# Preparing the first head pair of an attention kernel differently: sums by tensor, scaling on VectorE, joined turns, values loaded elsewhere, other dummies

## The chip, the cores and the metric

The kernel runs on one core of one Trainium2 chip. The metric is the device time of one execution in microseconds (us); lower is better. Each version is run several times and the median is taken. One further execution is recorded by the hardware profiler, and all views of the profile come from that one.

A core has a matrix engine (TensorE, PE in the profile, with PEld for its weight loads), VectorE (DVE), ScalarE (ACT), GpSimd (POOL) and SyncE (SP), which here only issues DMAs. Each engine works off its own instructions in program order and waits on semaphores for the others.

## The reference

An attention with normalised queries and keys (batch 8, 12 heads, 448 tokens, head dimension 64) is followed by a gated feed-forward block on 3584 tokens (model width 768, inner width 1536). Everything is float32.

```
q_n = q / sqrt(mean(q*q) + 1e-6) * g_q        # k_n likewise, with g_k
scores = q_n @ k_n.T / 8                      # per batch and head
attn   = softmax(scores)
x      = (attn @ v) as rows of 12*64 = 768
out    = (silu(x @ w_gate) * (x @ w_val)) @ w_out
```

The three weight matrices arrive in double precision, and the kernel converts them itself.

## The kernel before, in words

The program has a fast path (`fast`) and a general one that is entered only for unusual gains and is not used here. The fast path works on 48 pairs of heads: a pair is two heads of one batch. The first 12 pairs ("early", two batches) are done first, in an attention phase of their own. Then come four blocks of the feed-forward part, each for two batches. The blocks use a scheme with fewer products than the plain matrix product, so that inputs and weights are first combined into "sides" (line 1128 and 1132 for the inputs). The pairs of the next block are mixed into the present block.

In the attention phase each pair passes these steps. A pair's number is m; x is 0 for queries and 1 for keys.

- `load` (L748): one DMA each for queries and keys, rows of 112 partitions by 2 heads by 256 numbers, issued by SP. Four such tiles exist, so pair m+2 waits until pair m's tiles are free.
- `load_values` (L771, L774): four DMAs for the values, issued by SP. Two buffers.
- `square` (L784): ACT squares each tensor, 112x512.
- `summed` (L804): one DVE reduction, 112x1024 to 112x16, for both tensors.
- `inverse_root` (L698, L699 on ACT; L704 to L706 on DVE): Ln and Exp give an estimate of one over the root, and three small DVE operations improve it.
- `scale` (L843): two GpSimd products, 112x512, keys first.
- `turn` (L869): four PE transposes for each tensor into one PSUM tile of two banks (`st`).
- `drain`: keys on DVE (L875), queries on ACT with the gains `gg` as scale (L877).
- `scores` (L927) on PE and `exps` (L942) on ACT, in four parts j = 3, 0, 1, 2, where part 3 is half as wide. Two PSUM tiles `st` are shared by these and the turns.
- `weighted` (L1003) and `total` (L1034) on PE, then `copy_sums` (L1092, ACT), `join` (L1095, DVE), `invert` (L1070, L1072), `exchange` (L1085, ACT), `spread` (L1089) and `divide` (L1098).

Beside this, the first seven of 24 weight tiles are converted. A conversion (`convert`) has five DMAs (L1215, L1217), two ACT passes of 128x1152 (L1225, L1229), nine DVE operations in three parts (L1246, L1252, L1258), twelve GpSimd operations (L1279, L1282) and a DMA back to device memory (L1307).

The order of the instructions is made by a planner in plain Python, the class `Order`. Each step is added as a piece with its engine, a listed cost, a due time (`when`), the pieces that it comes after, the buffers that it takes and uses, and sometimes `early`, the time ahead of its due time from which it may start. The due time less a `rank` is its key. The early pairs have rank 60, the first weight conversions rank 20. `run` keeps a clock for each engine by the listed costs. It takes next the piece that can start first, with the key deciding between near ones, and emits it. So a changed cost or dependency can change the order of everything after it. DMAs are modelled with eight outstanding places. In the constants `LEAD` is 10.6 and `PAIR` 8.97: pair m has `base` = 10.6 + 8.97 m and `ready` = `base` - 8.97.

Ahead of the planned part, `fast` emits some steps by hand (from L1683): memsets on GpSimd, the table load on ACT (L570), four small gain loads on GpSimd's queue (L1692, L1693), the identity for the transposes, and a planned DVE product for the gains (L1697). A small check of the gains runs before that (L1748 to L1753). Pair 0's first square emits three extra PE products that nothing reads ("dummies", L787).

The dependencies that the planner does not model are found when the instructions are built: an instruction waits for earlier ones that touch the same memory, and for a PSUM tile the whole tile counts as seen in the trace.

Of the kernel before, what the change touches and what calls it, by code (L numbers as in the profile page):

```python
# [13 lines left out]
ALU = mybir.AluOpType  # L14
AX = mybir.AxisListType
# [477 lines left out]
def fast(  # L493
# [41 lines left out]
    nc = tc.nc  # L535
    B, H, S, D = q.shape
    DM = H * D
    DFF = moe_w_gate.shape[1]
    P = 128
    NJ = 4  # L540
    Q = S // 2
# [12 lines left out]
    VALUE_MOVES = [transfer(384, 256)] * 2 + [transfer(128, 256)] * 2  # L554
    NATURAL = (0, 1, 2, 3, 4, 5, 6, 7, 8, 9, 10, 11)
    R = S // NJ
# [9 lines left out]
        rr=4, ws=2, **{x + str(i): 1 for x in "vw" for i in range(6)},  # L566
# [5 lines left out]
    order = Order(dict(BUFS, bits=1), dict(logarithms=load_tables))  # L572
    tiles = {}
# [112 lines left out]
    GAIN = 2.0**24  # L686

    SCALE = 2.0**8
# [34 lines left out]
    def attention(m):  # L723
# [14 lines left out]
        def add(*what, **more):  # L738
            return order.add(*what, rank=rank, **more)
# [33 lines left out]
            for p in (0, D):  # L773
                nc.sync.dma_start(x[ds(p, D), NJ - 1], rows)  # L774

        load_v = add("SP", 2.4, ready - 16.0, load_values, takes=[("v", m)], moves=VALUE_MOVES, early=25.0)

        def square(x):
            if x == 0:
                take("t", m, [R, 2, 2 * NJ * D] if natural else [P, 2, NC, C])  # L780
            of = tiles["qk", (m, x)]
            if natural:
                of = of.rearrange("p h f -> p (h f)")
            nc.scalar.activation(tiles["t", m][:, x], of, AF.Square)  # L784
            if m == 0 and x == 0:
                for _ in range(3):
                    nc.tensor.matmul(banks[0], ident[0:R], of, start=True, stop=True)  # L787

        squares = []
        for x in range(2):  # L790
# [5 lines left out]
                )  # L796
            )


        def summed():  # L800
            if natural:
# [19 lines left out]
        def both():  # L821
# [2 lines left out]
                ss[:, 0], ss[:, 0], D * 1e-6, ss[:, 1], op0=ALU.add, op1=ALU.add  # L824
            )

        sums = add(
            "DVE", 1.45 if natural else 1.08, ready - 17.0, summed, after=squares, uses=[("t", m)], takes=[("ss", m)]
        )
        if not natural:  # L830
            sums = add("ACT", 0.88, ready - 16.0, swap, after=[sums], uses=[("ss", m)])
# [7 lines left out]
        def scale(x):  # L839
            if natural:  # L840
                split = dict(h=2, j=NJ, d=D)
                rr = tiles["rr", m][:, ts(x, 2 * NJ)].rearrange("p (h j one) -> p h j one", h=2, one=1)
                nc.gpsimd.tensor_tensor(  # L843
                    out=tiles["t", m][:, x].rearrange("p (j h d) -> p h j d", **split),
                    in0=tiles["qk", (m, x)].rearrange("p h (j d) -> p h j d", d=D),
                    in1=rr.to_broadcast([R, 2, NJ, D]), op=ALU.mult,
                )
                return
            rr = tiles["rr", m][:, ts(x, NC)].rearrange("p (c one) -> p c one", one=1)
            nc.gpsimd.tensor_tensor(  # L850
                out=tiles["t", m][:, x], in0=tiles["qk", (m, x)], in1=rr.to_broadcast([P, NC, C]),
                op=ALU.mult,
            )

        scaled = [
            add(
                "POOL", 0.98, ready - 9.0, lambda x=x: scale(x), after=[rr], port=True,
                uses=[("qk", (m, x)), ("t", m), ("rr", m)],
            )
            for x in (1, 0)  # L860
# [3 lines left out]
        def turn(x):  # L864
            if x:
                take("st", (m, "turned"), [P, 2, TB])
            turned = tiles["st", (m, "turned")][:, x]
            for j in range(NJ):
                nc.tensor.transpose(turned[:, ts(j, R)], tiles["t", m][:, x, ts(j, P)], ident[0:R, 0:R])  # L869

        def drain(x):
            turned = tiles["st", (m, "turned")][:, x, 0:S].rearrange("p (j r) -> p r j", j=NJ)
# [16 lines left out]
        kt = qt = None  # L889
        if natural:  # L890
            of_turned = ("st", (m, "turned"))
            for x in (1, 0):
                qt = add(
                    "PE", 0.4, ready - 6.0, lambda x=x: turn(x), after=[scaled[1 - x], qt],
                    uses=[("t", m)] + [of_turned] * (1 - x), takes=[of_turned] * x, mode="full",
                )
                kt = kt or qt
            kt = add(
                "DVE", 0.62, ready - 5.0, lambda: drain(1), after=[kt], takes=[("KT", m)],
                uses=[of_turned],  # L900
            )
            qt = add(
                "ACT", 0.63, ready - 5.0, lambda: drain(0), after=[qt, gains], takes=[("QT", m)],
                uses=[of_turned],
            )
        kt = kt or add(
            "DVE", 0.64, ready - 6.0, lambda: transpose(1), after=scaled[:1], takes=[("KT", m)],
            uses=[("t", m)],
# [771 lines left out]

    nc.gpsimd.memset(many, SCALE)  # L1683
    nc.gpsimd.memset(little, D * 1e-6 * GAIN**-2)
    nc.gpsimd.memset(halves, 0.0)
    for x in range(2):
        nc.gpsimd.memset(halves[ds(D * x, D), x], SCALE)
    load_tables()
    order.mode["ACT"] = "logarithms"
    for t, x in ((gq2, g_q), (gk2, g_k)):  # L1690
        col = x.rearrange("(d one) -> d one", one=1)
        nc.gpsimd.dma_start(t[0:64, :], col)  # L1692
        nc.gpsimd.dma_start(t[64:128, :], col)  # L1693
    make_identity(nc, ident)
    gains = order.add(
        "DVE", 0.2, 9.0,
        lambda: nc.vector.scalar_tensor_tensor(  # L1697
            out=gg, in0=gq2, scalar=8.0 * GAIN**-2, in1=gk2, op0=ALU.mult, op1=ALU.mult
        ),
        early=0.0,  # L1700
    )
    for m in range(EARLY):
        attention(m)
    first = [(up_weights, i) for i in range(4 * NG)] + [(down_weights, i) for i in range(2 * NG)]
# [83 lines left out]
```

## Time and profile before

| What | Value |
|---|---|
| time, three runs | 1462.16, 1462.22, 1463.76 us (median 1462.22) |
| profiled execution, its own time | 1464.89 us |
| its span, first to last instruction | 1463.1 us |
| PE busy | 1429.7 us (98%) |
| DVE busy | 881.6 us (60%) |
| ACT busy | 605.4 us (41%) |
| POOL busy | 398.3 us (27%) |
| granted PE clock, mean | 0.994 |
| DMA | 193.28 MB, mean 132 GB/s |

How to read the views that follow. A line of a group or of the timeline has the start in us and the busy time in us (timeline), the engine, the line of the code, the operation, the tile written and the tiles read, the shapes, and the count after an x. In square brackets stands how long the engine idled just before, and who released it. In the table by stage each row is a stretch of time, with each engine's busy time and, in brackets, its number of instructions; then the granted PE clock as a share of the full one, the share of time the DMA engines were busy, and the rate in GB/s. A line of the waits gives the waiting engine and line, whom it waited for, the total in us, how often, and the longest. "issue" means that nothing in the profile explains the idle time. Matmul ends are modelled.

### The profile page before, as it was taken

What the parts mean: (1) busy time and instruction counts of PE and PEld (TensorE: products, weight loads), DVE (VectorE), ACT (ScalarE), POOL (GpSimd) and SP (SyncE); (2) the same over time, 40 slices, a digit from 0 to 9 for tenths busy, and PEclk for the clock granted to TensorE, in tenths of its full rate; (3) what the DMA queues carried; (4) which work ended last, traced back from release to release, by engine and by line L of the source; (5) the groups of instructions that cost most, each with busy time, mean ns of one, the idle gap of its engine ahead of it and who ended that gap; (6) DMA issues with size and microseconds to landing.
All of it is one profiled execution on the core that took longest, in us unless ns stands there. A gap on an engine that the chain in (4) does not pass through costs nothing.

```text
span 1463.1 us, 19387 instructions
## 1 busy us (share of the span) xinstructions
PE 1429.7 (98%) x6726; PEld 685.1 (47%) x6726; DVE 881.6 (60%) x1493; ACT 605.4 (41%) x1222; POOL 398.3 (27%) x471
## 2 busy tenths in 40 slices
PE   6998999999999999999999999999999999999997
PEld 2443555544444455544444455554444445555553
DVE  3889977867866444446767632365676643432533
ACT  5885543457563221355654222254656322122100
POOL 3555786535343000012434200012344300000000
PEclk9999999999999999999999999999999999999999
DMA  7667998954454523443553532453454452322235
GB/s 209 185 189 254 337 313 285 297 139 92 102 103 96 133 72 109 110 101 87 118 116 71 118 99 75 117 118 84 103 116 87 96 134 73 102 78 81 78 99 108
DMA packets 410415, 193.28 MB, mean 132 GB/s; under 512 B 280004, under 2 KB 390852, under 8 KB 410308
## 3 DMA queue, kind: packets, MB, share of 16 engines
q1 hardware_dynamic: 399040, 190.57, 48.3%
q10 hardware_dynamic: 11140, 1.38, 0.7%
q8 instruction: 55, 0.90, 0.3%
q14 instruction: 52, 0.43, 0.1%
q0 software_dynamic: 128, 0.00, 0.0%
HBM read 157.29 MB, written 34.60 MB: 131 GB/s over the span
## 4 chain that ended last, share of the span: by engine, by line
PE 90%; DVE 3%; ACT 2%; DMA 2%; issue 1%; SPq 1%; POOL 0%; DVEq 0%; ACTq 0%; POOLq 0%
PE mm L1416 25%; PE at L1416 25%; PE mm L1594 23%; PE st L927 8%; PE at L1003 7%; PE st L1034 1%; ACT es L942 1%; PE mm L1034 1%; DMA out_dram<-spare 1%; DMA work<-in_k_dram 1%; DVE xs L1132 0%; PE st L869 0%; DMA xs<-in_moe_w_gate_dram 0%; DVE spare L1642 0%; DVE mm L1252 0%
## 5 line engine op out<-in xcount | busy, mean ns | idle before, releaser
L1416 PE MATMUL mm<-xs,ws 128*128 128x448 f32 x960 | 400.3, 540 | 0.0
L1416 PE MATMUL at<-xs,ws 128*128 128x448 f32 x960 | 400.2, 539 | 0.0
L1416 PEld LDWEIGHTS at<-xs,ws 128*128 128x128 f32 x960 | 182.3, 190 | 178.9 <-issue 174.7
L1416 PEld LDWEIGHTS mm<-xs,ws 128*128 128x128 f32 x960 | 182.4, 190 | 178.8 <-issue 174.1
L850 POOL TENSOR_TENSOR work<-work,rr 128x448 f32<-128x448 f32 x72 | 67.0, 952 | 468.6 <-DVE rr L706 381.9
L1594 PE MATMUL mm<-gt,ws 128*128 128x448 f32 x448 | 176.1, 544 | 0.0
L927 PE MATMUL st<-work 64*64 64x448 f32 (+1 forms) x1536 | 157.6, 517 | 13.7 <-ACT es L942 6.2
L942 ACT ACTIVATE es<-st 128x896 f32<-128x896 f32 x129 | 114.1, 913 | 110.5 <-PE at L1003 94.1
L1594 PE MATMUL mm<-hs,ws 128*128 128x448 f32 x384 | 151.8, 546 | 0.0
L1354 DVE TENSOR_TENSOR gt<-gt,mm 128x448 f32<-128x448 f32 x64 | 39.8, 621 | 184.3 <-PE mm L1416 182.8
L947 POOL TENSOR_TENSOR sums<-es 128x896 f32<-128x896 f32 x36 | 77.5, 2153 | 184.2 <-PE st L1034 111.2
L1594 PEld LDWEIGHTS mm<-gt,ws 128*128 128x128 f32 x448 | 83.5, 190 | 83.2 <-issue 81.7
L1490 ACT ACTIVATE st<-gt 128x448 f32<-128x448 f32 x96 | 52.6, 547 | 164.9 <-DVE gt L1358 82.0
L1352 ACT COPY gt<-mm 128x448 f32<-128x448 f32 x80 | 42.5, 531 | 167.4 <-PE mm L1416 167.2
L1003 PE MATMUL at<-es,v 64*64 64x448 f32 x1032 | 109.0, 538 | 2.6 <-DVE xs L1095 2.6
L1594 PEld LDWEIGHTS mm<-hs,ws 128*128 128x128 f32 x384 | 71.5, 191 | 72.9 <-issue 71.8
L927 PEld LDWEIGHTS st<-work 64*64 64x64 f32 x1536 | 51.9, 136 | 86.8 <-issue 40.1
L1352 ACT COPY v<-at 128x448 f32<-128x448 f32 x96 | 50.9, 530 | 76.4 <-PE at L1416 74.0
L947 POOL TENSOR_TENSOR sums<-sums,es 128x896 f32<-128x896 f32 x36 | 75.2, 2089 | 2.8
L1003 PEld LDWEIGHTS at<-es,v 64*64 64x64 f32 x1032 | 40.1, 134 | 61.5 <-issue 54.5
L784 ACT ACTIVATE work<-work 128x448 f32<-128x448 f32 (+1 forms) x96 | 55.2, 587 | 25.8 <-DMA work<-in_q_dram 17.1
L1354 DVE TENSOR_TENSOR v<-v,at 128x448 f32<-128x448 f32 x64 | 39.7, 621 | 41.2 <-PE at L1416 41.2
(160 smaller groups left out, 1566.9 us busy)
## 6 DMA issues: line engine op xcount, KB each, us to landing
ws<-up_sides SPq DMA_DIRECT2D x32, 1024.0 KB, 5.6
ws<-down_sides SPq DMA_DIRECT2D x16, 1024.0 KB, 5.7
ws<-down_sides SPq DMA_DIRECT2D x28, 512.0 KB, 4.6
ws<-up_sides SPq DMA_DIRECT2D x16, 768.0 KB, 4.8
out_dram<-spare SPq DMA_DIRECT2D x168, 56.0 KB, 2.1
v<-in_v_dram SPq DMA_DIRECT2D x96, 96.0 KB, 2.6
ws<-up_sides SPq DMA_DIRECT2D x32, 256.0 KB, 5.9
ws<-up_sides SPq DMA_DIRECT2D x16, 512.0 KB, 5.8
```

Of the source, the lines that this page charges most:

```text
L784: nc.scalar.activation(tiles["t", m][:, x], of, AF.Square)
L850: nc.gpsimd.tensor_tensor(out=tiles["t", m][:, x], in0=tiles["qk", (m, x)], in1=rr.to_broadcast([P, NC, C]), op=ALU.mult,)
L927: nc.tensor.matmul(st[ds(D * x, D), h, 0:n], tiles["KT", m][rows, ds(P * j + D * of_keys, D)], tiles["QT", m][rows, ds(Q * of_queries, n)] ...
L942: nc.scalar.activation(e, tiles["st", (m, j)][:, :, 0 : S * width(j) // P], AF.Exp)
L947: nc.gpsimd.tensor_tensor(out=to, in0=tiles["e", (m, 0)] if j == 1 else to, in1=e, op=ALU.add)
L1003: nc.tensor.matmul(tiles["at", (m, x)][ds(D * h, D), queries], tiles["v", m][rows, j, h], tiles["e", (m, j)][rows, h], start=j == 0, stop= ...
L1034: nc.tensor.matmul(to[ds(D * h + C * x, C)], halves[:, x] if half else many[:, 0:C], term[:, h, 0:Q] if half else term[:, h, ts(x, Q)], st ...
L1352: nc.scalar.copy(to, ps)
L1354: nc.vector.tensor_tensor(out=to, in0=old, in1=ps, op=ALU.add)
L1416: nc.tensor.matmul(ps(), w[:, which, c, at], xs[:, SLOT[x], c], start=fresh and c == 0, stop=c == NC2 - 1, skip_group_check=True,)
L1490: nc.scalar.activation(take(*act, [P, 2, TB])[:, 0, 0:S], to, AF.Silu)
L1594: nc.tensor.matmul(banks[s][:, 0:S], w[:, s, g, at], where[x][:, g], start=fresh and g == 0, stop=g == NG - 1, skip_group_check=True,)
```

## The change

All of it concerns the start of the program. The diff is complete but for unchanged lines.

- Values: the load of an early pair's values is due at `base` - 2 instead of `ready` - 16, and may start 4 us ahead of that instead of 25.
- Dummies: the three products behind pair 0's first square go. Instead DVE clears half of the tile `more`, and PE multiplies it with itself, four times with 448 columns and once with 224 columns, at the start. A further product of 224 columns follows pair 0's turn of the queries.
- Pair 0's sums of squares are two DVE reductions of 112x512, one for each tensor. Pair 1's reduction must come after pair 0's drain of the keys.
- Pair 0 is scaled by DVE instead of GpSimd, with a listed cost of 0.62 instead of 0.98.
- Pair 0's two turns are one piece, emitted one behind the other.
- The gains' product is two GpSimd operations, emitted by hand behind the memsets and the identity, and no planned piece; GpSimd's memsets come behind its DMA issues.

```diff
-        load_v = add("SP", 2.4, ready - 16.0, load_values, takes=[("v", m)], moves=VALUE_MOVES, early=25.0)
+        load_v = add(
+            "SP", 2.4, base - 2.0 if early else ready - 16.0, load_values, takes=[("v", m)], moves=VALUE_MOVES,
+            early=4.0 if early else 25.0,
+        )
...
             nc.scalar.activation(tiles["t", m][:, x], of, AF.Square)
-            if m == 0 and x == 0:
-                for _ in range(3):
-                    nc.tensor.matmul(banks[0], ident[0:R], of, start=True, stop=True)
...
+        def summed_half(x):
+            if x == 0:
+                take("ss", m, [P, 2, 2 * NC])
+            nc.vector.tensor_reduce(
+                out=tiles["ss", m][0:R, 0, ts(x, 2 * NJ)],
+                in_=tiles["t", m][:, x].rearrange("p (n d) -> p n d", d=D), axis=AX.X, op=ALU.add,
+            )
...
-        sums = add(
-            "DVE", 1.45 if natural else 1.08, ready - 17.0, summed, after=squares, uses=[("t", m)], takes=[("ss", m)]
+        sums = None
+        for x in range(2 if m == 0 else 0):
+            sums = add(
+                "DVE", 0.65, ready - 17.0, lambda x=x: summed_half(x), after=[squares[x], sums],
+                uses=[("t", m)] + [("ss", m)] * x, takes=[("ss", m)] * (1 - x),
+            )
+        sums = sums or add(
+            "DVE", 1.45 if natural else 1.08, ready - 17.0, summed,
+            after=[*squares, clusters.get("turned") if m == 1 else None], uses=[("t", m)], takes=[("ss", m)]
         )
...
-                nc.gpsimd.tensor_tensor(
+                engine = nc.gpsimd if m else nc.vector
+                engine.tensor_tensor(
                     out=tiles["t", m][:, x].rearrange("p (j h d) -> p h j d", **split),
...
-                "POOL", 0.98, ready - 9.0, lambda x=x: scale(x), after=[rr], port=True,
+                "POOL" if m else "DVE", 0.98 if m else 0.62, ready - 9.0, lambda x=x: scale(x),
+                after=[rr], port=True,
...
                 nc.tensor.transpose(turned[:, ts(j, R)], tiles["t", m][:, x, ts(j, P)], ident[0:R, 0:R])
+            if m == 0 and x == 0:
+                warm(Q)
...
-            for x in (1, 0):
+            for xs_of in ((1, 0),) if m == 0 else ((1,), (0,)):
                 qt = add(
-                    "PE", 0.4, ready - 6.0, lambda x=x: turn(x), after=[scaled[1 - x], qt],
-                    uses=[("t", m)] + [of_turned] * (1 - x), takes=[of_turned] * x, mode="full",
+                    "PE", 0.4 * len(xs_of), ready - 6.0, lambda xs_of=xs_of: [turn(x) for x in xs_of],
+                    after=[scaled[1 - xs_of[-1]], qt], mode="full",
+                    uses=[("t", m)] + [of_turned] * (1 - xs_of[0]), takes=[of_turned] * xs_of[0],
                 )
...
+            clusters.setdefault("turned", kt)
...
-    nc.gpsimd.memset(many, SCALE)
-    nc.gpsimd.memset(little, D * 1e-6 * GAIN**-2)
-    nc.gpsimd.memset(halves, 0.0)
-    for x in range(2):
-        nc.gpsimd.memset(halves[ds(D * x, D), x], SCALE)
+    def warm(n):
+        nc.tensor.matmul(banks[0][:, 0:n], more[:, 0, 0:P], more[:, 0, 0:n], start=True, stop=True)
+
+    nc.vector.memset(more[:, 0], 0.0)
+    for n in (S, S, S, S, Q):
+        warm(n)
     load_tables()
...
+    nc.gpsimd.memset(gg, 8.0 * GAIN**-2)
+    nc.gpsimd.memset(little, D * 1e-6 * GAIN**-2)
+    nc.gpsimd.memset(many, SCALE)
+    nc.gpsimd.memset(halves, 0.0)
+    for x in range(2):
+        nc.gpsimd.memset(halves[ds(D * x, D), x], SCALE)
     make_identity(nc, ident)
-    gains = order.add(
-        "DVE", 0.2, 9.0,
-        lambda: nc.vector.scalar_tensor_tensor(
-            out=gg, in0=gq2, scalar=8.0 * GAIN**-2, in1=gk2, op0=ALU.mult, op1=ALU.mult
-        ),
-        early=0.0,
-    )
+    nc.gpsimd.tensor_tensor(out=gg, in0=gq2, in1=gg, op=ALU.mult)
+    nc.gpsimd.tensor_tensor(out=gg, in0=gg, in1=gk2, op=ALU.mult)
+    gains = None
```

## The prediction

> **What bounds the kernel now.** I read the page first: TensorE (PE) is busy 1429.7 of 1463.1 us. So only its 33 us of idle time, and the time it spends at half clock, can be won. I then asked for busy time by stage, cutting where the chain of work that ended last changes its engine.
>
> ```profile
> core 0: us, PE busy (x) PEld busy (x) DVE busy (x) ACT busy (x) POOL busy (x), PEclk, DMA share, GB/s
> 0.00:30.68 30.68, 19.44 (x86) 7.75 (x90) 9.84 (x22) 15.51 (x27) 11.11 (x23) 0.90 0.74 200
> 30.68:97.50 66.82, 65.78 (x821) 31.90 (x813) 53.85 (x112) 59.37 (x112) 36.94 (x59) 1.00 0.67 198
> 97.50:130.20 32.70, 26.76 (x292) 11.72 (x292) 31.07 (x58) 22.27 (x37) 17.71 (x32) 0.95 0.65 214
> 134.72:1463.10 1328.38, 1313.19 (x5473) 631.66 (x5472) 782.73 (x1296) 506.94 (x1041) 328.28 (x353) 1.00 0.48 125
> ```
>
> The start (to 30.68) loses 11.2 us of PE. From there to 97.5 PE is full. From 97.5 to 130.2 VectorE (DVE) is full instead and PE loses 5.9 us. The rest is PE again. What the start loses moves everything behind it, if the DVE stage lets it through. Next I read the timeline of pair 0:
>
> ```profile
> 3.78 1.35 ACT L784 ACTIVATE work<-work 112x512 f32<-112x512 f32 x2 [0.91 <-DMA work<-in_q_dram]
> 5.16 1.22 DVE L804 TENSOR_REDUCE ss<-work 112x16 f32<-112x1024 f32 x1 [0.87 <-ACT work L784]
> 6.81 0.63 ACT L784 ACTIVATE work<-work 112x512 f32<-112x512 f32 x1 [1.68 <-DMA work<-in_q_dram]
> 7.70 0.63 ACT L784 ACTIVATE work<-work 112x512 f32<-112x512 f32 x1 [0.26 <-DMA work<-in_k_dram]
> 8.24 0.29 ACT L698 ACTIVATE rr<-ss,little 112x16 f32<-112x16 f32 x1
> 8.36 1.22 DVE L804 TENSOR_REDUCE ss<-work 112x16 f32<-112x1024 f32 x1 [1.98 <-ACT work L784]
> 9.50 0.17 DVE L704 SCALAR_TENSOR_TENSOR ss<-ss,rr 112x16 f32<-112x16 f32 x1
> 10.23 2.04 POOL L843 TENSOR_TENSOR work<-work,rr 112x512 f32<-112x512 f32 x2 [5.98 <-ACT rr L699]
> 12.37 0.62 DVE L875 COPY work<-st 128x448 f32<-128x448 f32 x1 [2.12 <-PE st L869]
> 13.14 0.98 PE L869 MATMUL st<-ident,work 112*128 112x112 f32 x4 [0.81 <-DVE ss L704]
> 14.16 0.63 ACT L877 ACTIVATE work<-st,gg 128x448 f32<-128x448 f32 x1 [3.99 <-PE st L869]
> 14.85 1.77 PE L927 MATMUL st<-work 64*64 64x224 f32 x12 [0.72 <-ACT work L877]
> ```
>
> Pair 0's sums are ready at 6.38, yet its Ln (L698) stands on ACT behind both squares of pair 1, which wait for their loads, until 8.24. Its improvement (L704) then stands on DVE behind pair 1's reduction until 9.50. The second turn (13.14) starts only 0.15 after the first drain ends (12.99), although its input is ready at 12.27: it waits for that drain's reading of the common PSUM tile. Last, what follows:
>
> ```profile
> 20.28 1.26 ACT L1225 ACTIVATE xs<-xs 128x1152 f32<-128x1152 f32 x1
> 21.43 0.91 ACT L942 ACTIVATE es<-st 128x896 f32<-128x896 f32 x1
> 25.20 0.90 ACT L942 ACTIVATE es<-st 128x896 f32<-128x896 f32 x1
> 26.15 4.76 PE L927 MATMUL st<-work 64*64 64x448 f32 x24 [3.15 <-ACT es L942]
> 27.00 0.65 DVE L704 SCALAR_TENSOR_TENSOR ss<-ss,rr 112x16 f32<-112x16 f32 x1 [0.68 <-ACT rr L699]
> PE at L1003 <- DVE xs L1095: 3.7, 2, 2.6
> ```
>
> Pair 1's scores (26.15) wait for pair 0's last Exp on ACT (25.20), which stands in an ACT queue that runs from 19.75 with one gap of 0.32. Before that ACT idles: 10.17 to 14.16, 14.79 to 15.94, 16.48 to 17.43, 18.35 to 19.75, in all 7.5 us. The last line is PE waiting in the DVE stage for a join (L1095).
>
> [...] the row of L1354 has 621; [...] L804 has 1.22 us. So 512 elements cost an estimated 0.69 us. [...] The timeline has 2.04 us for two, against an estimated 1.38, a ratio of 1.5[...]. [...] L704 takes 0.65 at 27.00, inside GpSimd's 26.58 to 28.62, and 0.17 elsewhere. [...] PE idles from 23.0 to 26.15, and the clock is 0.50 from 24.4 to 31.2; eight transposes (L869) take 1.75 at 17.30 and 0.99 at 31.80 (at 17 the clock column says 1.00; there I go by the durations).
>
> **The change, part by part.** Times are the profiled execution's.
>
> Sums by tensor: one reduction of 1.22 becomes two of 0.69. The first runs beside the second square, so the sums end near 5.86 instead of 6.38. By the planner's costs in the code, Ln now falls between pair 1's two squares: its sums come before the second one's load. Those squares wait for real loads (6.79, 7.68), so Ln starts after the first, near 7.4. Before, the last square's start to Exp's end was 8.78 - 7.70 = 1.08; so 6.81 + 1.08 = 7.89. Gain 0.9; the earlier sums alone are worth nothing here.
>
> Pair 1's reduction put after pair 0's key drain: improvement starts at 7.95 instead of 9.50 and ends at 8.53. Gain 1.55 so far. Behind the new wait on DVE stand that reduction, then pair 1's improvement; GpSimd's scaling of pair 1 waits for them. I get 15.3 instead of 13.62 for it. But pair 1's turn started at 17.30 only, held by PE, so this is covered by 1.6 us. Without cover it costs up to 1.7.
>
> Scaling on DVE: 8.55 to 9.95, two of 0.69, instead of 1.85 for GpSimd's first turn plus the wait. The bounds are 0.62 (planner's cost) and 1.02 (GpSimd's) each. GpSimd does nothing then but two 128x1 products for the gains[...].
>
> Both turns together: they run 9.3 to 11.1 cold (eight took 1.75 in pair 1), or to 10.5 warm. Then the DVE drain, 0.62, and the ACT drain, 0.63, which in pair 1 waits for the DVE one (19.75 after 19.71); with the hand-overs, scores at 12.5 cold, 11.9 warm, against 14.85. Gain 2.3 to 2.9; I take 2.5.
>
> Dummies: four products of 448 and one of 224 columns. The old dummy's 512-column half costs 0.85, so these cost 4 x 1.5 + 0.75 = 6.7, from some 1.2 to 7.9[...]. Turns start at 9.3: hidden by 1.4. The one behind the turns (0.75) is hidden by the drains (1.25). DVE's new memset (not in the trace; between 0.1 and a copy's 0.62) is hidden before 3.66.
>
> Gains on GpSimd: DVE loses 0.16; the gains' last load landed near 8.3 and the ACT drain needs them at 11.2: hidden by 2.9, at nothing. GpSimd's memsets behind its four DMA issues: identity still by 4.5, nothing.
>
> Values: eight DMAs (2.69 to 8.30) leave SP's queue ahead of the first weights; pair 0's four go behind the first weight load's five, pair 1's four behind the second weight load's five and pair 2's queries and keys. Later pairs keep their buffers' release as their start; only rank falls, and the 11 us from a release (34.91) to the use (46.1) covers it. Weights 0 are issued from 2.7 instead of 8.34 and land near 10 to 11.5; queries 2 at 11.3 instead of 14.80.
>
> So ACT finds weights 0 ready when the query drain ends, and the first conversion step (1.26) and the second big Exp (0.91) fall into the 7.5 us of idle ACT: 2.2 less in the queue in front of 25.20. Sum: 2.5 + 2.2 = 4.7 us earlier at pair 1's scores. Not counted: if the idle of 23.0 to 26.15 closes, the 5 us of PE work to 31.2 runs at full clock, up to 2.5 more.
>
> The profiled execution (1464.9) would become 1460.2, its span 1458.4. It lies 2.7 above the median, in which I see only scatter; the median 1462.2 becomes 1457.5.
>
> **Rivals.** First, more: the cold stretch goes (2.5) and conversions begun earlier relieve the full DVE stage, up to half its 5.9: 4.7 + 2.5 + 2.5 gives 1452.5. For it: 14 us of conversion steps (25 of 0.56: L1246, L1252, L1258) lie in that stage while DVE idles 21 us before 30.68. Against: each conversion has low rank and ACT is 89% busy from 30.68 to 97.5. Second, nothing: the DVE stage is a queue with its own length; an earlier PE arrives at the same queue, and 0.5 of 4.7 remains: 1461.7. For it: 31.07 of 32.70 busy. Against: DVE is idle 13 us in the stage ahead, so its queue is fed by what moves. Third, slower: the planner re-orders all with new times, and on DVE's queue of 97.5 to 130.2 conversions come ahead of the joins that PE waits for. A conversion is 9 x 0.56 = 5.0 us. One eats the gain, so it decides from the second on: 4.7 less 10.0, 1467.5. For it: the present 2.6 us wait behind six such steps. Against: joins rank higher.
>
> **Numbers.** About 0.2%, 2.9 us, is what a measurement here can tell from no change: below 1459.3 is faster, above 1465.1 slower. Forecast 0.55, more 0.12, nothing 0.20, slower 0.13. Faster 0.67, same 0.20, slower 0.13. The range 1452.5 to 1463.0 takes in the first three and leaves out the slower case and the edges, about 0.2; the forecast's own is 1455 to 1459.
>
> **What would show it.** First scores at 11.9 to 12.5; Ln of pair 0 between pair 1's squares; weight conversion (L1225) near 12; pair 1's big scores near 21.5; no half clock from 24 to 31; the first block product 4 to 5 us before 134.72. I am wrong if weights 0 land after 12.7, so that ACT stands in front of the Exps, or if the DVE stage grows by what the start saves.

## The result and the profile after

The changed kernel takes 1466.86 us (median of nine runs), the kernel before 1462.22 (median of nine, beside it); one of the nine executions of the changed kernel, at 3635.6 us, fell in a much slower state and is left out of the ratio. The ratio is 1.0029, 95% interval 1.0017 to 1.0040: slower by about 0.3%, where 1457.5 and "faster" were forecast. The profiled execution takes 1466.87 us with a span of 1465.1, 2.0 more than the span before. The medians differ by 4.6. The other 2.7 us lie with the kernel before, whose profiled execution (1464.89) took that much longer than its median here; timed again beside the experiments below, it had medians of 1464.0 to 1464.8. The changed kernel was timed on the first occasion only, so its loss may be nearer 2 to 3 us than 4.6. The traces show the 2.0.

The start did become faster. This is the timeline of pair 0 in the kernel after (start, busy time, engine, line, operation, idle time before it and its releaser). Lines have moved: L784 is now L787, L804 is L803 and L812, L843 L859, L869 L886, L875 L894, L877 L896, L927 L948, L942 L963, L1225 L1246, L1229 L1250.

```profile
7.56 0.63 ACT L787 ACTIVATE work<-work 112x512 f32<-112x512 f32 x1 [2.69 <-DMA work<-in_q_dram]
8.10 0.29 ACT L698 ACTIVATE rr<-ss,little 112x16 f32<-112x16 f32 x1
8.54 0.61 ACT L787 ACTIVATE work<-work 112x512 f32<-112x512 f32 x1
8.67 0.18 DVE L704 SCALAR_TENSOR_TENSOR ss<-ss,rr 112x16 f32<-112x16 f32 x1 [3.08 <-ACT rr L699]
9.30 1.31 DVE L859 TENSOR_TENSOR work<-work,rr 112x512 f32<-112x512 f32 x2
10.15 1.28 PE L886 MATMUL st<-ident,work 112*128 112x112 f32 x8 [2.06 <-DVE work L859]
11.47 0.62 DVE L894 COPY work<-st 128x448 f32<-128x448 f32 x1 [0.86 <-PE st L886]
12.19 0.63 ACT L896 ACTIVATE work<-st,gg 128x448 f32<-128x448 f32 x1 [3.04 <-DVE work L894]
12.72 1.24 ACT L1246 ACTIVATE xs<-xs 128x1152 f32<-128x1152 f32 x1
12.88 5.27 PE L948 MATMUL st<-work 64*64 64x224 f32 x32 [0.67 <-ACT work L896]
```

The Ln (8.10) stands between pair 1's two squares (7.56, 8.54), DVE scales at 9.30, both turns come together at 10.15, and the first scores start at 12.88 instead of 14.85: 2.0 earlier. The first conversion pass starts at 12.72 instead of 20.28. Pair 0's `total` starts at 23.2 instead of 34.8, pair 8's at 99.7 instead of 103.2. Yet the first product of block 0 comes at 136.89, not 134.66. Busy time by stage of the kernel after, at the cuts of the prediction:

```profile
0.00:30.68 30.68, 24.93 (x180) 11.71 (x180) 15.45 (x36) 19.20 (x34) 10.01 (x24) 0.89 0.82 223
30.68:97.50 66.82, 62.03 (x760) 28.24 (x764) 50.72 (x103) 57.53 (x113) 35.26 (x56) 1.00 0.63 189
97.50:130.20 32.70, 25.50 (x265) 9.73 (x256) 30.61 (x55) 17.33 (x29) 20.42 (x33) 0.90 0.56 174
136.89:1465.10 1328.21, 1313.30 (x5476) 631.51 (x5472) 783.65 (x1296) 506.92 (x1041) 325.87 (x350) 1.00 0.47 125
```

The first column behind the duration is PE. The start wins 5.5 us of PE time (24.93 against 19.44), of which 2.2 are only longer dummies (7.7 against 5.5); the pairs' stage loses 3.75 (62.03 against 65.78), and the third row 1.26. The third column is DVE: up to 30.68 it is 5.6 us busier than before (1.31 of it is the scaling that GpSimd did), then up to 97.5 it does 3.1 less (50.72 against 53.85). So little of the earlier start became earlier DVE work. PE's waits up to 140 in the kernel after (total, times, longest):

```profile
PE at L1024 <- DVE xs L1116: 7.8, 3, 4.6
PE st L948 <- ACT work L896: 4.0, 7, 1.0
```

The first line was 3.7 before: PE waits for the joins on DVE (L1116, before L1095). The second was 1.5 in three times, so it is new in this size: in the new order, scores come straight behind the pair's own two drains, seven times.

The stretch from pair 8's `total` to block 0's first product is called the hand-over below. It takes 31.46 us in the kernel before and 37.19 after. The two rows, kernel before and then kernel after:

```profile
103.20:134.66 31.46, 25.57 (x299) 10.78 (x297) 30.04 (x55) 18.09 (x31) 17.68 (x32) 0.95 0.62 202
```

```profile
99.70:136.89 37.19, 29.06 (x301) 11.36 (x297) 33.94 (x61) 18.91 (x32) 24.27 (x40) 0.86 0.59 197
```

DVE is busy 30.04 of 31.46 and 33.94 of 37.19. The same chain bounds both. In the kernel before DVE improves pair 11's root (L704) at 99.56 and ends the last join at 130.17. After, the two are at 99.85 and 131.07. Kernel before, then kernel after:

```profile
99.56 0.18 DVE L704 SCALAR_TENSOR_TENSOR ss<-ss,rr 112x16 f32<-112x16 f32 x1
129.56 0.61 DVE L1095 TENSOR_TENSOR xs<-xs,at 128x448 f32<-128x448 f32 x1
```

```profile
99.85 0.62 DVE L704 SCALAR_TENSOR_TENSOR ss<-ss,rr 112x16 f32<-112x16 f32 x1
101.50 1.14 DVE L1153 TENSOR_TENSOR xs<-xs 128x448 f32<-128x448 f32 x2
102.67 1.35 DVE L1149 SCALAR_TENSOR_TENSOR xs<-xs 128x448 f32<-128x448 f32 x1
103.95 2.12 DVE L1153 TENSOR_TENSOR xs<-xs 128x448 f32<-128x448 f32 x2
130.46 0.61 DVE L1116 TENSOR_TENSOR xs<-xs,at 128x448 f32<-128x448 f32 x1
131.94 2.61 PE L1024 MATMUL at<-es,v 64*64 64x448 f32 x12
```

PE is 3.5 us ahead at pair 8, but DVE, whose queue decides, is 0.3 behind at the same step, with the same 26 conversion steps still to do. The stretch on DVE takes 31.2 instead of 30.6. The side operations (L1149, L1153) are part of that: the first six take 5.3 us, 4.1 before. GpSimd scales pair 11 beside them, from 101.27 to 104.93 (before, from 100.40 to 102.60, where one of the six took 0.99). Where the two overlap, both are slower: one side operation alone takes 0.62 (the mean of 52 later ones), two of the six take 1.35 and 1.46, and GpSimd's two products take 2.28 and 1.42 instead of 1.02. The last join thus ends 0.90 later; from there to block 0 PE needs 5.82 us instead of 4.49, since its clock is halved at 130.4 while it waits (0.50 until 133.8; the twelve products from 131.94 take 2.61, those from 130.66 in the kernel before 1.66). 0.90 + 1.33 = 2.23 us, the whole difference at block 0 in these two executions.

### The profile page after: what moved, and what is told of

Read it like the earlier page. It is cut to its first block, busy times and chain, and to the rows that moved or that the text cites. A ratio compares the mean times of both kernels' runs of the same rounds, so it can differ in the third digit from the quotient of the medians.

```text
span 1465.1 us, 19402 instructions
## 1 busy us (share of the span) xinstructions
PE 1431.5 (98%) x6732; PEld 683.6 (47%) x6732; DVE 885.4 (60%) x1496; ACT 604.7 (41%) x1222; POOL 397.5 (27%) x472
## 3 DMA queue, kind: packets, MB, share of 16 engines
q10 hardware_dynamic: 11140, 1.38, 0.7%
## 4 chain that ended last, share of the span: by engine, by line
PE 90%; DVE 4%; ACT 3%; DMA 1%; issue 1%; SPq 0%; POOL 0%; ACTq 0%; DVEq 0%; POOLq 0%
PE mm L1437 25%; PE at L1437 25%; PE mm L1615 23%; PE st L948 7%; PE at L1024 7%; PE st L1055 1%; ACT es L963 1%; DMA out_dram<-spare 1%; PE mm L1055 1%; PE st L886 1%; DVE xs L1153 0%; DVE mm L1273 0%; DMA work<-in_q_dram 0%; DVE work L894 0%; ACT work L896 0%
## 5 line engine op out<-in xcount | busy, mean ns | idle before, releaser
L948 PE MATMUL st<-work 64*64 64x448 f32 (+1 forms) x1536 | 154.0, 509 | 11.8 <-ACT work L896 4.0
L963 ACT ACTIVATE es<-st 128x896 f32<-128x896 f32 x129 | 114.3, 914 | 111.0 <-PE at L1024 94.5
L1024 PE MATMUL at<-es,v 64*64 64x448 f32 x1032 | 112.3, 549 | 5.5 <-DVE xs L1116 5.5
L948 PEld LDWEIGHTS st<-work 64*64 64x64 f32 x1536 | 50.0, 133 | 88.0 <-issue 39.3
L787 ACT ACTIVATE work<-work 128x448 f32<-128x448 f32 (+1 forms) x96 | 55.3, 586 | 24.4 <-DMA work<-in_q_dram 16.9
```

Source lines behind the costliest of these rows:

```text
L948: nc.tensor.matmul(st[ds(D * x, D), h, 0:n], tiles["KT", m][rows, ds(P * j + D * of_keys, D)], tiles["QT", m][rows, ds(Q * of_queries, n)] ...
L963: nc.scalar.activation(e, tiles["st", (m, j)][:, :, 0 : S * width(j) // P], AF.Exp)
L1024: nc.tensor.matmul(tiles["at", (m, x)][ds(D * h, D), queries], tiles["v", m][rows, j, h], tiles["e", (m, j)][rows, h], start=j == 0, stop= ...
```

## The experiments

Four theories stand against each other; the expectations name some of them by letter. Q: the hand-over has its own length, whatever comes earlier. O: the planner's new order of PE's work for the pairs loses it. W: the delay by the new wait on DVE loses it directly. C: what decides is how much DVE work, chiefly conversion steps of 0.56 us, is left when pair 8's `total` comes, and the planner's new order leaves too much. The table is read from each kernel's profiled execution (us); hand-over and DVE in it are the row of busy times from pair 8's `total` to block 0. Ratios are to the kernel before run beside it, with the 95% interval. Each trace is one execution: `after` and `after_cut` have the same start, and their first scores differ by 0.5 us.

| kernel | ratio | first scores | `total` of pair 8 | hand-over | DVE busy in it | conversion steps left | block 0 |
|---|---|---|---|---|---|---|---|
| before | 1 | 14.85 | 103.2 | 31.46 | 30.04 | 26 | 134.66 |
| after | 1.0029 (1.0017 to 1.0040) | 12.88 | 99.7 | 37.19 | 33.94 | 26 | 136.89 |
| frozen | 0.9994 (0.9985 to 1.0003) | 12.04 | 100.6 | 31.42 | 30.00 | 26 | 132.02 |
| before_cut | 0.9973 (0.9965 to 0.9981) | 14.52 | 102.1 | 24.65 | 15.38 | left out | 126.75 |
| after_cut | 0.9958 (0.9945 to 0.9971) | 12.37 | 99.8 | 26.66 | 18.22 | left out | 126.46 |
| after_nowait | 0.9928 (0.9910 to 0.9945) | 13.97 | 100.0 | 25.01 | 23.28 | 14 | 125.01 |
| before_values | 0.9954 (0.9939 to 0.9969) | 15.65 | 100.4 | 29.68 | 26.95 | 19 | 130.08 |
| after_early2 | 0.9938 (0.9918 to 0.9959) | 12.86 | 102.3 | 23.62 | 19.61 | 11 | 125.92 |
| after_sides_pool | 0.9973 (0.9962 to 0.9983) | 12.70 | 99.7 | 30.74 | 26.48 | 25 | 130.44 |
| nowait_sides_pool | 0.9919 (0.9902 to 0.9935) | 14.12 | 101.1 | 22.52 | 18.95 | 13 | 123.62 |
| nowait_values_back | 0.9994 (0.9985 to 1.0002) | 12.31 | 105.0 | 31.14 | 29.89 | 23 | 136.14 |

### The new preparation in the old order (frozen)

The new preparation of pair 0, with its wait, but emitted by hand at the old places, so that the planner's order of everything else stays that of before. The values are not moved.

```diff
-                nc.gpsimd.tensor_tensor(
+                (nc.gpsimd if m else nc.vector).tensor_tensor(
...
+            if m == 0:
+                if x:
+                    take("st", (m, "turned"), [P, 2, TB])
+                    for y in (1, 0):
+                        turn_one(y)
+                    warm(Q)
+                return
...
+                if m == 0:
+                    stash["sums"]()
```

> The kernel before with its order of all later instructions kept, and the new preparation of pair 0 put in by hand: sums by tensor, scaling on VectorE, joined turns, new dummies, gains on GpSimd, Ln of pair 0 ahead of pair 1's second square, pair 1's reduction behind pair 0's key drain. Values stay where they were. Theory Q (the VectorE queue at the handover to block 0 takes up what the start wins): first scores near 12.5 instead of 14.85, first block product within 1 us of 134.7, time 1461 to 1463. Theory O (the re-planned order of the later pairs is what loses): with the old order the start's gain passes, first block product 131 to 132.5, time 1459 to 1460.

First scores at 12.04 instead of 14.85, block 0 at 132.02 instead of 134.66: 2.64 of 2.8 us arrive. The hand-over has the same length, the same DVE work and starts earlier. Block 0 is where O had it (131 to 132.5). So Q falls in its strong form: the queue takes its time from whenever it begins, and in the old order it begins earlier with the start (pair 11's improvement is at 96.93, in the kernel after at 99.85). The whole time hardly moves, though, and its median of 1463.1 is near what Q had: the ratio is 0.9994, between 2.2 us less and 0.4 more. About 1 us of the traced gain is given back behind block 0, where this trace has more time at half clock than the kernel before (mean clock 0.89 against 0.94 from 300 to 330 us; last section).

### Without the conversion steps of three tiles (before_cut, after_cut)

```diff
+    CUT = [("up", i) for i in (4, 5, 6)]
...
-                    "DVE", 0.76 if by_bank else 0.53, when, lambda k=k, op=op: op(k),
+                    "DVE", 0.76 if by_bank else 0.53, when, lambda k=k, op=op: None if key in CUT else op(k),
```

> The kernel before, order and listed costs kept, with the 27 VectorE operations left out that round the weight tiles 4, 5 and 6 (15 us of VectorE; these weights stay unrounded, so the output is not the reference's). Theory Q: the stage from 97.5 to 130.2 is no longer full of VectorE work, PE's 5.9 us of idle time there go, first block product 129 to 131, time 1456 to 1459. Theory O: also earlier, since PE waits for joins there; it is the base for the next run.

> The changed kernel, order and listed costs kept, with the same 27 VectorE operations left out as in the run before_cut (output not the reference's). Theory Q: without the queue the 5 us that PE is ahead at pair 7 come through, first block product 4 to 5 us earlier than in before_cut, time 4 us under before_cut. Theory O: the loss sits in the order of the pairs, so it stays: within 1 us of before_cut or slower.

These kernels leave out 27 DVE operations and with them the rounding of three weight tiles. That shortens the hand-over by 6.8 us in the kernel before and by 10.5 in the one after, to 24.65 and 26.66; block 0 then comes at nearly the same time (126.75 and 126.46). So DVE work bounds the hand-over in both kernels, by more than Q had for before_cut (129 to 131). Less arrives at the end: from block 0 to the last product before_cut takes 1323.2 us, the kernel before 1321.0. O keeps a part: without the DVE bound the changed order should bring its 2 us of lead at the first scores to block 0 (Q had 4 to 5 there), and brings 0.3; the time is 2.4 us under before_cut, between the two theories.

### Without the new wait (after_nowait)

```diff
-            after=[*squares, clusters.get("turned") if m == 1 else None], uses=[("t", m)], takes=[("ss", m)]
+            after=squares, uses=[("t", m)], takes=[("ss", m)]
```

> The changed kernel without the rule that pair 1's reduction comes after pair 0's key drain; the planner orders anew, and by its own costs block 0 begins 6 us sooner, though pair 0's totals come 8 us later than in the changed kernel. Theory Q: what the start wins or loses does not matter, what the planner's order leaves for VectorE at the handover does: first scores 1 to 2 us later than the changed kernel's 12.9, first totals after 28, and yet first block product 129 to 132, time 1458 to 1462. Theory W (the new wait delays pair 1 and that is the loss): pair 1's scaling starts before 14, the totals of pair 0 come no later than 23.2, and the time falls by the same 1 to 2 us all the way. Theory O: the time follows the pairs' period: under 8.6 us between totals if it is faster.

The best single edit: 0.9928, with block 0 earlier than any theory had it (125.01; Q 129 to 132). And it is not because the pairs run sooner. Pair 1's scaling does start 1.0 earlier (14.16), but the first scores come 1.1 later than in the changed kernel (13.97), pair 0's `total` at 32.4 instead of 23.2, pair 8's at 100.0 instead of 99.7. This rules out W as the cause. What differs is where ACT takes the first weight tiles. These are ACT's first four conversion passes (two for a tile) in the kernel after, and then without the wait:

```profile
12.72 1.24 ACT L1246 ACTIVATE xs<-xs 128x1152 f32<-128x1152 f32 x1
20.60 1.27 ACT L1250 ACTIVATE xs<-xs 128x1152 uint32<-128x1152 uint32 x1
37.81 1.29 ACT L1246 ACTIVATE xs<-xs 128x1152 f32<-128x1152 f32 x1
46.66 1.28 ACT L1250 ACTIVATE xs<-xs 128x1152 uint32<-128x1152 uint32 x1
```

```profile
11.72 1.23 ACT L1246 ACTIVATE xs<-xs 128x1152 f32<-128x1152 f32 x1 [2.74 <-DMA v<-in_v_dram]
13.82 1.26 ACT L1250 ACTIVATE xs<-xs 128x1152 uint32<-128x1152 uint32 x1
17.57 1.26 ACT L1246 ACTIVATE xs<-xs 128x1152 f32<-128x1152 f32 x1
24.98 1.27 ACT L1250 ACTIVATE xs<-xs 128x1152 uint32<-128x1152 uint32 x1
```

Tile 1's passes come at 17.57 and 24.98 without the wait, at 37.81 and 46.66 with it, and in the kernel before at 35.46 and 44.65:

```profile
35.46 1.31 ACT L1225 ACTIVATE xs<-xs 128x1152 f32<-128x1152 f32 x1
44.65 1.28 ACT L1229 ACTIVATE xs<-xs 128x1152 uint32<-128x1152 uint32 x1
```

By pair 8's `total`, near 100 us in both, ACT has begun 10 passes in the kernel after and 13 without the wait. With the wait the planner fills ACT's early time with the Exps of pairs 0 and 1 instead. DVE has then done 9 conversion steps by 40 us, against 18 without the wait, and 38 against 49 by pair 8's `total`. The hand-over without the wait, and PE's wait for the joins up to 140:

```profile
100.00:125.01 25.01, 23.03 (x299) 10.13 (x297) 23.28 (x43) 15.36 (x29) 11.58 (x21) 1.00 0.59 190
```

```profile
PE at L1024 <- DVE xs L1116: 1.3, 1, 1.3
```

DVE has 10.7 us less to do, PE waits 6.5 less, and its clock stays at 1.00.

### The values' place alone (before_values)

The kernel before, with the load of the values changed and nothing else.

```diff
-        load_v = add("SP", 2.4, ready - 16.0, load_values, takes=[("v", m)], moves=VALUE_MOVES, early=25.0)
+        load_v = add(
+            "SP", 2.4, base - 2.0 if early else ready - 16.0, load_values, takes=[("v", m)], moves=VALUE_MOVES,
+            early=4.0 if early else 25.0,
+        )
```

> The kernel before with one part of the change alone: the values' load moved (due at base - 2, early 4). The order is planned anew. Theory C (what decides is how many VectorE conversion steps are left when the total of pair 8 comes; 26 in both kernels, 14 in after_nowait, 0.56 us each): the first weights come sooner, ACT's passes over weight tiles 0 and 1 fall into its idle start, some 20 steps are left, first block product near 130, time 4 to 5 us under before. Theory W (the new wait, and nothing else in the change, costs): no wait here, so only the earlier loads count; within 1 us of before. Theory O (PE's order in the pairs): the period of the totals stays as before, no change.

0.9954: alone, this part makes the kernel faster. Tile 1's passes come at 24.9 and 34.5 instead of 35.5 and 44.7, 19 steps are left instead of 26, and block 0 comes 4.6 us earlier although the first scores are 0.8 later.

### The first two conversions ranked up, with the wait (after_early2)

```diff
-        rank = 0.0 if by_bank else 20.0
+        rank = 0.0 if by_bank else 60.0 if key[1] < 2 else 20.0
```

> The changed kernel, new wait and all, with the first two weight conversions at rank 60 (as the early pairs) instead of 20, so that their steps come early. Theory C: some 11 to 14 steps are left at the total of pair 8, 7 to 8 us less VectorE work at the handover; pairs 1 to 8 run later by 4 to 6 us; first block product 130 to 132 instead of 136.9, time 1459 to 1462 where the changed kernel has 1467. Theory W: the wait is still there, so pair 1 is as late as before and the time stays at 1466 or above. Theory O: conversions among the pairs lengthen the period of the totals to 9 us and over, and that adds up to a slower kernel.

The wait stays, but tile 1's passes come at 24.0 and 25.2. 11 steps are left, the hand-over takes 23.62, the ratio is 0.9938. So neither the wait itself nor another part of the change forces the loss: moving the conversions is enough to undo it. The pairs pay for it (pair 8's `total` at 102.3, 2.6 later), and it still gains 11 us at block 0, more than C had (130 to 132).

### Side operations on GpSimd (after_sides_pool, nowait_sides_pool)

Eight of eleven side operations for block 0's first part go to GpSimd; the second kernel leaves the wait out as well.

```diff
+            engine = "POOL" if op is not None and n == 0 and c == 0 else "DVE"
...
-                    "DVE", 0.62, when,
-                    lambda to=x[i], one=x[one], two=x[two], op=op: combined(to, one, two, op),
+                    engine, 0.95 if engine == "POOL" else 0.62, when,
```

> The changed kernel with eight of the eleven operations for block 0's first sides on GpSimd instead of VectorE (listed cost 0.95); nothing is left out. This takes 8 x 0.75 = 6 us from VectorE at the handover, where GpSimd is half idle. Theory C, widened to all VectorE work at the handover: first block product 132 to 134 instead of 136.9, time 1462 to 1464. Theories W and O: the loss is made before the handover and PE's order stays, so at most 1 us.

> after_nowait (the fastest so far, 1452.7) with the same eight operations on GpSimd. Theory C: VectorE's stage shortens further, first block product 121.5 to 123.5 instead of 125.0, time 1449 to 1451. [...]

With the same pair times as in the changed kernel (`total` of pair 8 at 99.7) and other DVE work taken away, the hand-over shortens by 6.5 us for 7.5 us less of DVE (block 0 at 130.44, sooner than C's 132 to 134): not the conversions as such count, but the DVE time. Without the wait the same edit wins less (2.5 us for 4.3), and the ratio 0.9919 can't be told from 0.9928. PE is now busy 22.4 of 22.52 us, so it is the bound again. Slower DVE operations beside GpSimd's have a part too: the side operations left on DVE take 0.97 (L1149) and 0.87 us (L1153), against 0.72 and 0.75 in after_nowait, and GpSimd is busy 21.51 of the 22.52 us of the hand-over, there 11.58 of 25.01. So block 0 comes near C's figure (123.62), but the time, 1452.1, misses C's 1449 to 1451. In this one trace, besides, the stretch behind the last product is 10.3 us against 7.4.

### Without the wait, with the values at their old place (nowait_values_back)

The kernel after_nowait, with the edit of before_values taken back.

```diff
-            "SP", 2.4, base - 2.0 if early else ready - 16.0, load_values, takes=[("v", m)], moves=VALUE_MOVES,
-            early=4.0 if early else 25.0,
+        load_v = add("SP", 2.4, ready - 16.0, load_values, takes=[("v", m)], moves=VALUE_MOVES, early=25.0)
```

> The changed kernel without the new wait on pair 1's reduction, and with the values loaded at the old place. Theory C (the DVE work left when the total of pair 8 comes sets the hand-over): what made the version without the wait fast is that the first weight tiles arrive and are converted early, and that needs the values out of their way on SP's queue; with the values back, some 20 to 24 of the 0.56 us conversion steps are left at the total of pair 8 instead of 14, the first block product comes at 130 to 132 instead of 125.0, and the ratio to the kernel before is 0.997 to 1.000. Rival P (the rewritten preparation without the wait is enough by itself, whatever the values do): 14 steps left, the first block product near 125 to 126, ratio 0.993.

The ratio, 0.9994, and the 23 steps left are what C expects, and P falls. Block 0 at 136.14 is 4 us later than C's figure: pair 8's `total` comes at 105.0. Tile 0's first pass waits until 31.7, and the pairs lose 4.75 us of PE time (busy 69.15 of 73.9) before the hand-over, which with 29.89 us of DVE takes the expected 31.14. So the preparation wins nothing measurable without the values' move: 0.9994 without it, 0.9954 with the move alone, 0.9928 with both and no wait (the intervals of these two overlap), 1.0029 with both and the wait.

### Parts of the preparation, in the fixed order

Each was run once, on the frozen kernel; their times (1462.5, 1463.1, 1463.9, and 1463.2 for frozen's profiled execution) lie within the scatter, so only the traces are read.

```diff
-                (nc.gpsimd if m else nc.vector).tensor_tensor(
+                nc.gpsimd.tensor_tensor(
```

> The fixed order with pair 0's scaling back on GpSimd. From the durations (1.29 us for two on DVE, 2.04 for two on GpSimd) the turns, which begin after the second product, start 0.75 us later, so first scores at 12.8 instead of 12.04. Since the order is fixed, the first block product moves by the same 0.75, to 132.8, if nothing behind absorbs it; if the hand-over has a length of its own, it stays at 132.0.

```diff
-                    warm(Q)
...
-    for n in (S, S, S, S, Q):
-        warm(n)
```

> The fixed order without any dummy products (the clearing of half of the tile stays). If the dummies are what makes pair 0's eight transposes run at full rate (1.0 us for eight, against 1.75 for eight cold ones), the turns take 0.75 us more and the first scores, themselves at half rate, start at 12.8 and the pair's first products take twice as long; first block product 0.7 to 2 us later than 132.0. If the clock is up at that time anyway, nothing moves.

```diff
-                    for y in (1, 0):
-                        turn_one(y)
+                turn_one(x)
+                if not x:
```

> The fixed order with pair 0's key turn, key drain, query turn, query drain one behind the other, instead of both turns together. If the second turn has to wait for the first drain's reading of the common PSUM tile, the chain is turn 0.5, drain 0.64, turn 0.5, drain 0.64 instead of turn 1.1, drain 0.64, drain 0.64: with joined turns the two drains run one after the other too, so only the hand-overs differ, and the first scores come 0.1 to 0.4 later, near 12.3; the first block product moves by the same. If the joined turns alone save a whole drain, it is 0.7 later.

Turns and first scores of frozen, then of frozen_no_dummies, then of frozen_turns_apart:

```profile
9.48 1.11 PE L902 MATMUL st<-ident,work 112*128 112x112 f32 x8 [1.40 <-DVE work L866]
12.04 1.36 PE L962 MATMUL st<-work 64*64 64x224 f32 x16 [1.05 <-ACT work L912]
```

```profile
9.13 1.73 PE L901 MATMUL st<-ident,work 112*128 112x112 f32 x8 [9.13 <-DVE work L866]
12.30 2.52 PE L961 MATMUL st<-work 64*64 64x224 f32 x16 [1.45 <-ACT work L911]
```

```profile
9.45 0.57 PE L902 MATMUL st<-ident,work 112*128 112x112 f32 x4 [1.84 <-DVE work L866]
10.07 0.62 DVE L908 COPY work<-st 128x448 f32<-128x448 f32 x1 [0.15 <-PE st L902]
10.75 1.01 PE L902 MATMUL st<-ident,work 112*128 112x112 f32 x4 [0.72 <-DVE work L908]
12.53 2.52 PE L962 MATMUL st<-work 64*64 64x224 f32 x16
```

Scaling on DVE is worth 0.70 us at the first scores (12.74 with GpSimd) and 0.88 at block 0 (132.90), near the 0.75 expected. Without dummies the turns take 1.73 instead of 1.11 and the first sixteen score products 2.52 instead of 1.36; as the loads came 0.36 earlier in this execution the scores start only 0.26 later, but pair 0's `total` 1.4 later (33.5 against 32.1). Turned apart, the query turn waits for the key drain and then runs at half rate (1.01 instead of 0.57): scores 0.49 later, `total` 1.8 later (33.9). The estimate of 0.1 to 0.4 had left out the clock, which is at half from 10.00 to 16.83 here and from 14.36 to 21.19 in frozen (the first sixteen score products take 2.52 here, 1.36 there); that the wait between the turns does this is a guess, not shown by one execution each. Block 0 comes at 135.10 and 135.46, 3.1 and 3.4 later, more than at `total`: PE falls to half clock at 129.3 and 129.5, while it waits for the last join (in frozen_no_dummies the twelve products from 129.48 take 3.18 us, and the mean clock of the hand-over is 0.90 against 0.95), and DVE is busy 30.74 and 31.61 us in the hand-over, 30.00 in frozen. In frozen's execution the clock did not fall at that place, so only the difference at `total` can be put down to the edits.

## Why the prediction was wrong

**The start: right, with smaller sizes.** Ln fell between pair 1's squares, at 8.10 instead of 7.4, because pair 1's queries landed at 7.54 instead of 6.79. The improvement ended at 9.27, not 8.53. DVE scaling took 1.31 for two, not 1.38: one took 0.71 and one 0.68, and they overlap. The estimate of 0.69 for 512 elements lies on a straight line through the prediction's two rows, a DVE product of 448 elements in 621 ns (L1354) and a reduction of 1024 in 1.22 us (L804); each of the two new reductions took 0.69 as well. Turns were warm at first (1.28 for eight; the clock is at half from 10.96 to 17.79); the drains ran one after the other. First scores 12.88, not 11.9 to 12.5: gain 2.0, not 2.5. In the fixed order it was 2.8.

**Covered costs: right.** The dummies ended at 8.09, before the turns at 10.15; the memset took 0.43 and the gains cost nothing. Pair 1's scaling started at 15.16 (15.3 forecast). Pair 2's queries were issued at 12.88, not 11.3.

**ACT's idle time: used, as forecast.** Weight tile 0's first pass came at 12.72, and pair 0's `total` even 11.6 earlier. Pair 1's big scores came at 20.76 (21.5 forecast), and the half clock of 24 to 31 went. Up to here the mechanism held.

**The step that failed is the passage through the DVE stage.** Against the rival "nothing" the prediction held that DVE "is idle 13 us in the stage ahead, so its queue is fed by what moves", and it carried 4.7 us to block 0. What moved was pair 0's and pair 1's PE and ACT work; the DVE work that fills the later stage is on converted weights, and apart from tile 0 these moved back: tile 1's passes from 35.46 and 44.65 to 37.81 and 46.66, and those of tiles 2 and 3 too. DVE therefore stood no further at pair 11's improvement than before (99.85 against 99.56), with the same 26 steps to do, and the 3.5 us that PE had won went into waits for joins (7.8 instead of 3.7) and half clock behind them (mean clock of the hand-over 0.86 instead of 0.95). So none of the 4.7 us arrived at block 0; it came 2.23 later, 0.90 by DVE (0.29 of it there already at 99.85, the rest with slower side operations) and 1.33 by the half clock at 130.4. In short, I took the planner's order as given and moved it; the change gave it a new one.

**The rivals.** The time is that of "slower" (1467.5), whose kernel of truth was that the planner re-orders everything. Its mechanism did not happen, so the number fits by chance: no conversion slid ahead of a join in the hand-over, and as many steps were left as before. "Nothing" had the right place, the DVE queue, but frozen shows that the queue lets a gain through when its content is unchanged. "More" named the very thing that the better versions do, conversions begun earlier relieving the DVE stage; the wait keeps the changed kernel from it. Its objection, that conversions have low rank and ACT is busy, was the right forecast for tile 1.

**Shown and open.** Shown: the wait, through the planner, costs about 1.0% (after against after_nowait, by their ratios); an earlier place of two conversions, with the wait kept, is enough to undo the loss (after_early2); DVE time left sets the hand-over (the cut kernels, the side operations). Open: which listed cost or key makes the planner choose so; where the changed order loses the 2.3 us of lead that after_cut has at pair 8's `total`; and why the kernel before was 2.7 us faster in the median of its first nine executions than in its trace. The whole change in the old order, values included, was not run.

The version to keep is after_nowait (0.9928) or, with side operations on GpSimd, nowait_sides_pool (0.9919); they can't be told apart, and the interval of after_early2 overlaps both.

## What to carry to other kernels

Where a planner makes the order, an edit at the start is two edits: the one in the diff and the new order of everything behind it; try the first in the old order, as in frozen, before pricing the second. Ask of a stage that an engine bounds what work is left on that engine when the stage begins: here 11 us less of DVE work made the hand-over 12 us shorter, while in the changed kernel scores 2 us earlier gave nothing. And a wait that protects one short chain can let a planner use the free time for the wrong thing: look where the work that feeds the later bound goes.

## What was not expected of the hardware

**A PE wait can cost more than itself.** In each of six traces (before, after, frozen, frozen_no_dummies, after_nowait, nowait_values_back) PE waits 2.7 us for an ACT drain once between 300 and 330 us. In some executions the clock is halved at its end or just behind it (to 0.50 at 318.0 in the kernel before, where the wait ends at 318.02, and at 321.6 in the one after, where it ends at 320.25); in others not (1.00 throughout in frozen_no_dummies and nowait_values_back). Busy times from 300 to 330 us in frozen and in frozen_no_dummies:

```profile
300.00:330.00 30.00, 27.30 (x106) 11.78 (x104) 21.74 (x37) 18.74 (x38) 7.91 (x6) 0.89 0.51 134
```

```profile
300.00:330.00 30.00, 27.31 (x114) 12.23 (x113) 21.95 (x37) 19.81 (x40) 7.89 (x6) 1.00 0.58 144
```

PE is busy equally long, with clock 0.89 against 1.00. What it costs is read from the same two steps in each: pair 13's improvement on DVE comes 186.9 us after block 0 in both, and the `total` of pair 12 behind it 201.7 in frozen, where the clock is at half for 6.8 us, and 198.7 in frozen_no_dummies, where it is not. The kernels before and after, with 3.4 us at half clock there, lie between (200.2 and 200.4). The 3.0 us are nearly all of the difference to the end: from block 0 to the last product frozen takes 1322.0 us, frozen_no_dummies 1318.8. So a gain of 2 to 3 us at block 0 can vanish in one execution and not in the next. What decides whether the clock falls there is not shown by these runs.

**Loads beside loads.** In the kernel after, weight tile 0's loads are issued from 2.70 instead of 8.34, and ACT can square pair 1's queries at 7.56. Two pairs of kernels differ in the values' place alone: with the values moved it is 7.27 instead of 6.81 (before_values, before) and 7.39 instead of 6.84 (after_nowait, nowait_values_back). Over all traces it is 6.55 to 7.18 with the values at the old place (seven) and 7.23 to 7.73 with the weights ahead of them (seven). So in these traces the move delays the queries by about half a microsecond; that it is the weights' traffic that does it is argued, not shown.
